# Sums of split mixing weights formed on chip instead of through a scratch tensor, with a new instruction order

## The chip, the cores and the metric

The kernel runs on one core of one Trainium2 chip. The metric is the device time of one execution in microseconds (us). Its engines are TensorE (PE in the profile; its weight loads are PEld), VectorE (DVE), ScalarE (ACT), GpSimd (POOL) and SyncE (SP), which here issues every DMA.

## The reference

The input is `q`, `k`, `v` of 4 batches, 8 heads, 768 positions and 64 columns per head. A local attention (window of 16, plus one key per block of 32 that is the block's maximum, with the block's mean as value) gives `x` of shape 4 x 768 x 512. Then:

```python
theta = x @ w_theta
zr, zi = x * cos(theta), x * sin(theta)
y = einsum('ts,bsd->btd', w_tok_r, zr) + einsum('ts,bsd->btd', w_tok_i, zi)
u = x + y
out = u + maximum(u @ w_ch, 0)
```

The four weights arrive as 64-bit floats and are converted to float32 on chip.

## The kernel before

**Stages.** A batch has 6 tiles of 128 positions, so there are 24 tiles. For one tile TensorE makes the scores (L523), VectorE masks them and takes the row maximum (L559), ScalarE takes the exponential (L563), TensorE transposes (L572) and multiplies by the values (L546), the result is normalised into `xn`, and TensorE turns it (L605) into `x`. The `theta` product is L639 for the first six tiles (plain float32) and L644 for the rest, where each operand is split into a high part that fits the fast matmul format and a low part with the remainder; three products then stand for one. The phases are L655 (ScalarE), L657 (VectorE), an absolute value (L661 or L663) and two sines (L667, L668), and L674 multiplies by `xn` into the tile pair `zu`. ScalarE loads a table whenever it changes between exponential and sine.

**Mixing.** `y` is a sum over 6 steps `s` of `zr`, `zi` times the weights `w_tok_r`, `w_tok_i` of that step. Batches 0 and 1 do it in L702 (first with plain `zu` and float32 weights, then with split operands `hl`). Batches 2 and 3 do it with seven products of half-size blocks, L817 (the function `mix_fast`). Four of the seven need sums of weight blocks. `weight_sums` makes these once: for each of six steps and two halves of the columns it builds a tile `f` with four quarters, does four small adds or subtractions in place (L730, 128 x 192 each), splits the result in high and low (L309/L311 and L318) and writes both to the DRAM tensor `s_scratch`. `mix_fast` streams them back into the second half of the six weight slots `wt`, one load for each step and product, 24 in each of the two batches.

**Where the sums start from.** In the kernel before, each step's whole float32 weights (both kinds, 768 KB) are written from their slot to the DRAM tensor `f_scratch` when they are converted, and `weight_sums` reads them back by halves of the columns (12 loads). Later the same weights are split into the slots `w_t[s, 0]` and `w_t[s, 1]`, high part and low part, for L702 and L817.

**End.** `swap_pools` closes the attention's memory pool; `channel_weights` and `out_batch` then do the last product, again with seven block products (L922), with corrections on VectorE (L929, L941) and one output DMA for each half row.

**Order.** Nothing is scheduled at run time. The constant `ORDER` lists all operations (2292 before) by number; a letter after a number names the engine where there is a choice (`g` GpSimd, `d` VectorE). Each engine carries out its own operations in this order and waits on semaphores for the others. Where a GpSimd operation that shares a port with VectorE stands directly after a VectorE operation of that kind in the list, it also waits for that one's end.

The operation that both the sums and the corrections use is

```python
def add_op(dst, x, y, n, sign, reads, writes, due, engines=("DVE", "POOL")):
```

Of the kernel before, what the change touches and what calls it, by code (L numbers as in the profile page):

```python
# [58 lines left out]
253 104 85 98 215 214 110 223 216 296g 258 224 99d 225 243 255 257 217 118 348g 226 105 227 218 119g 220d 293 256 245 219d 106
244 246 228 247 250 111 120 221 291 121 249 222d 248 123 124g 297 229 122 349g 298 345 259 230 260 262 292 299 261 270 130 125  # L60
301 350g 115 300 271 263 126 272 303 423g 305 302 304 306 273 267d 308 131g 307 116 264d 419 310 135 268 309 265 274 313 127
136g 132 311 312 266d 141 275 269d 314 276 133 315 142g 137 317 316 277 138 352 143 112 231 325 326 318 232 134 327 163 233g
139 144 353 361 168 319d 356 328 320 329 362 278 330 322 355 234 169g 145 331 346 164g 321d 279 364 323 363 282 117 146 324
283 420 332 354 113 347 284 280 365 474 285 147 380 358 114 357 339 165 360 148 366 359 337 166 367 338 149 167 170 368 150
152 381 424 369 422 333 370 400 153 382 128 383 384 171 334 154 172 155 157 281 158g 156 425 385 371 402 401 159 372 386 340
174 335 175g 373 426 392 394 374 421 160 375 377 376 378 387 529 161 404 176 388 379 403 705g 389 454 177 530 179 395 393 178
180 455 456 390g 472 408 457 181 405 182 410 183 427 703 458 459 414 466 409 412 460 461 462 463 411 435 428 467 429 704g 406
437 706g 438 415 431 430 441 468 615g 469 413 436 434 464g 707 521 442 433 465 432 416 417 407 479g 440 564d 523 443 439 480
288g 741 709g 534 444 446d 418 481 535 482 445 485 483 447 490 477 129 492 491 484 475 448 478g 493 486 496 449 451d 532 710g
452 743 450d 488 531g 522 453d 497 616g 487 536 509 537 539 494 586 476d 540 489 538 495 498 510 621 499 391g 501 543 500d 541  # L70
742 511 502 512 545 503 506 513 542 547 551 504 546 733 507 583 289g 286g 708g 549 505d 550 533g 343g 548 544 745 508d 514 744
552 553 515 341 554 555 524 516 556d 517 711 712 518 287g 713d 714 739 585 336g 557 344g 398 734 587 596 558d 599 519 624 588
603 559 715 592 589 716 746 717 561 668 568 591 562 565g 622 735 593 718 566 719 584 560d 597 140 601 720 595 563 598 567 600
602 399g 784 590 594 623 342 569 785d 604 473g 721 786 740 605 572 625 607d 570 634 606 576 608 626 635 787g 617 788 653g 722
618 665 638 151 789 629 574 697 637 630 396d 397g 470 619 525g 723g 737 639 627 790 698g 609d 620 636 628 520 832 612 633 736
471g 162 641 833g 654g 659g 613 738 834g 631 791 640 610 611d 632 792 614d 655 841 642 747 752 643 835g 669 526 644d 793 645
670 646 812 678 672 657 679 650 813d 671 173 667 683 681 658 814d 815 680 663 647d 836 673 748 842 816 675 664 684 843g 817
656 648 818 755 754 724 945g 837 674 682 844 819 660g 677 661 649d 651 666 527d 652 676 685 820 686 687 794 839 689 821 688d
795 838g 756 1015 757 690 528g 571 845g 975 765 662 822 759 760 976d 850 691 840 977d 578 846 978 851g 796 768 823 727d 763
184 797 852 946 699 766 758 692 853g 769 1020 701 694d 979 940 702 980 700 941 847g 772 848 693d 579 981 825 767 695 749 696d  # L80
761 762 771 731 753 750 764 580g 798d 824 982 728 770 732 773 983 774 775d 984 947 956 581g 776 854g 777 995 948 729 778d 959
849 781d 949 950 958 725g 582g 802 952 803 996 997 998 953 799g 859 751 943 1016 1021 779 951 782 855 999 730 780 1074 1000
985 860g 1001 856 800 726 963 1018 808 857 1002 942 954 861g 957 961 960 962 801 955 575 826g 783 964 862 863g 1077 858 944g
965 1003 1022 966 1004 986 967d 864g 968 1005 806 804 1017g 810 1031 972 868 805 865g 1050 828 1023 1051d 1052 1032 869g 573
577 987 829 1170 1053 830 1024 866 1025 1033 989g 1006 969d 1054 827 1035 1037 831 1029 1055 870 1028 993 871 1056 1007g 970
872g 1027 1034 867 973 1120d 1038 1008 877 994 1036 1026 1057 1019d 1058 1013 1030 971 1014 974d 873d 1059 1039 874g 1040 1042
1078 878 1041d 809 811 990g 1079 1043 1047d 1208 1076 807 1087 1089 991 876 992 1209 1088 1090 1011 1210d 1083 1094 1093 1044d
1060 879 1009 880 1211 1080 1212 875 881 1082 1129 1012 1045 882g 1048 1213 886 1061 1126 1081 1092 1066 883 1075 1010 884
1084 1091 1214 1063g 1085 887 1067 885 1062 1127 1121 1046d 988 888 1215 1086 1173 1068 1049 1216 895 1095 1096 1098 1106g
1130 1217 1097d 889 1099 1218d 1279 1107g 1280 1281g 1069 1131 1070 896 1071 1228 1133 1100d 1282 1064g 1219 1135 890 1103d  # L90
1229 1283 1072 1073 1139 1065 891g 1137 1132 1110 1141 892 1142 1101 1284 1111 897 1143 1104 1285 1134 1138 1102d 898g 1108
1105d 1145 899g 1146 1286 1140 1144 1136 1109 1287 1128 893 900d 1158d 1147 1148 901g 1150 894 1288 1172 1250 1149d 1118 1174
1289 1114 1175 1112 1151 1305 1116 1178 1179 902 1202 1236 1122 1152 1183 903 1221g 1123 1306 1124 1185 1307 1308g 1187 1177
1181 1309 1153 904 1182 1160 1184 1232 1310 1155 1189 1237 1230 1233 1220g 1188 1176 1125 1186 1311 905 1156 1162 1171 1290
# [1028 lines left out]
```

## Time and profile before

| | |
|---|---|
| runs | 436.08, 436.68 and 437.91 us (median 436.68) |
| profiled execution, first to last instruction | 435.6 us |
| profiled execution's own time | not listed apart; the median run is 1.1 us above the span |
| busy: PE, DVE, ACT, POOL | 421.7, 352.2, 280.3, 209.7 us |
| moved by DMA | 100.07 MB |

A row of a timeline gives start, duration, engine, line, operation, tiles, and in brackets the idle time just before it on its engine with what ended it; PE rows run into each other because matmuls are pipelined. A row of a group gives busy time, then the mean duration of one in ns, then idle time before them.

### The profile page before, as it was taken

How to read it: one execution, taken by the hardware profiler on the slowest of the kernel's cores; microseconds unless marked ns; L12 is line 12 of the kernel's file. 1: busy time of each engine (PE TensorE's matmuls, PEld its weight loads, DVE VectorE, ACT ScalarE, POOL GpSimd, SP SyncE). 2: the span in 40 equal slices, each digit the busy share in tenths (PEclk: the TensorE clock that was granted, in tenths of full speed). 3: DMA queues.
4: the chain of work that ended last, by engine and by line, in shares of the span. 5: the costliest groups of instructions: out<-in, count | busy, mean ns of one | idle time of the engine just before them, and what ended most of it. 6: DMA issues, size and time to landing. Idle time of an engine off the chain costs nothing.

```text
span 435.6 us, 10044 instructions
## 1 busy us (share of the span) xinstructions
PE 421.7 (97%) x3682; PEld 350.9 (81%) x3682; DVE 352.2 (81%) x947; ACT 280.3 (64%) x600; POOL 209.7 (48%) x208
## 2 busy tenths in 40 slices
PE   5989999998999999999999999999999989999996
PEld 1455555665888888888888899999899989999996
DVE  3799999778988777875757695866489989999996
ACT  1799995787757784866785885493955447455210
POOL 3543324687775665245465578624453410251542
PEclk9899999999999999999999999999999999999999
DMA  8999956989678678848767987883379696220138
GB/s 294 347 354 364 295 197 208 290 257 322 230 233 273 197 224 266 259 139 247 232 188 223 292 273 218 245 246 119 111 230 338 229 367 223 75 73 20 65 136 289
DMA packets 76321, 100.07 MB, mean 230 GB/s; under 512 B 23024, under 2 KB 58864, under 8 KB 76272
## 3 DMA queue, kind: packets, MB, share of 16 engines
q1 hardware_dynamic: 76272, 99.43, 71.1%
q8 instruction: 29, 0.48, 0.5%
q14 instruction: 20, 0.16, 0.1%
HBM read 75.82 MB, written 23.59 MB: 228 GB/s over the span
## 4 chain that ended last, share of the span: by engine, by line
PE 87%; DMA 10%; DVE 1%; ACT 1%; SPq 0%; issue 0%; POOL 0%; DVEq 0%
PE m L702 25%; PE m L817 19%; PE t L644 11%; PE c L922 7%; PE m L922 6%; PE pa L546 5%; PE s L523 4%; PE t L639 3%; PE t L605 3%; DMA q<-qg 3%; PE pa L572 3%; DMA wth<-wth 2%; DMA wt<-wti 2%; DMA zu<-kT 2%; DMA wt<-s_scratch 1%; PE t L922 1%
## 5 line engine op out<-in xcount | busy, mean ns | idle before, releaser
L817 PE MATMUL m<-wt,hl 128*128 128x384 f32 x504 | 95.7, 339 | 1.4 <-DMA wt<-s_scratch 1.2
L817 PEld LDWEIGHTS m<-wt,hl 128*128 128x128 f32 x504 | 87.7, 188 | 4.9 <-ACT hl L309 1.5
L702 PE MATMUL m<-wt,hl 128*128 128x512 f32 (+1 forms) x432 | 84.9, 341 | 0.0
L702 PEld LDWEIGHTS m<-wt,hl 128*128 128x128 f32 x432 | 68.6, 188 | 10.8
L563 ACT ACTIVATE e<-e,st 128x118 f32<-128x118 f32 x192 | 63.1, 388 | 12.1 <-DVE st L559 11.6
L559 DVE CUSTOM_DVE_ANT_0 e<-s,cs 128x118 f32<-128x118 f32 x192 | 46.8, 272 | 9.6 <-PE s L523 4.7
L318 POOL TENSOR_TENSOR hl<-zu,hl 128x512 fp32r<-128x512 f32 x23 | 30.1, 1309 | 43.9 <-DMA wt<-s_scratch 15.9
L644 PE MATMUL t<-wth,xh 128*128 128x512 f32 x144 | 45.3, 396 | 0.0
L674 POOL TENSOR_TENSOR zu<-xn,zu 128x512 f32<-128x512 f32 x20 | 27.0, 1350 | 20.3 <-ACT zu L668 5.5
L657 DVE SCALAR_TENSOR_TENSOR zu<-zu,t 128x512 f32<-128x512 f32 x24 | 16.4, 684 | 24.4 <-ACT zu L655 24.4
L702 PE MATMUL m<-wt,zu 128*128 128x512 f32 (+1 forms) x96 | 33.4, 491 | 1.2 <-DVE zu L674 1.2
L655 ACT ACTIVATE zu<-t,bmagic 128x512 f32<-128x512 f32 x24 | 16.5, 687 | 23.9 <-PE t L644 18.3
L309 ACT CAST hl<-zu 128x512 fp32r<-128x512 f32 x31 | 19.1, 619 | 18.2 <-PE m L817 14.9
L702 PEld LDWEIGHTS m<-wt,zu 128*128 128x128 f32 x96 | 17.5, 190 | 15.8 <-issue 12.6
L546 PEld LDWEIGHTS pa<-v,e 118*64 118x64 f32 x768 | 24.8, 137 | 6.8 <-issue 3.0
L318 DVE TENSOR_TENSOR hl<-zu,hl 128x512 fp32r<-128x512 f32 x37 | 27.6, 751 | 2.3 <-ACT hl L309 2.1
L523 PE MATMUL s<-k,q 64*64 64x118 f32 x768 | 25.6, 272 | 3.9 <-POOL cs L340 3.2
L546 PE MATMUL pa<-v,e 118*64 118x65 f32 x768 | 28.1, 224 | 1.2 <-ACT e L578 1.2
L730 POOL TENSOR_TENSOR zu<-zu 128x512 f32<-128x512 f32 x15 | 21.4, 1432 | 15.0 <-DVE zu L730 4.9
L644 PE MATMUL t<-wth,xl 128*128 128x512 f32 x72 | 28.6, 397 | 0.0
L674 DVE TENSOR_TENSOR zu<-xn,zu 128x512 f32<-128x512 f32 x28 | 24.7, 884 | 4.8 <-ACT zu L668 4.6
L523 PEld LDWEIGHTS s<-k,q 64*64 64x64 f32 x768 | 20.2, 135 | 9.2 <-POOL cs L343 4.0
(181 smaller groups left out, 909.9 us busy)
## 6 DMA issues: line engine op xcount, KB each, us to landing
wt<-s_scratch SPq DMA_DIRECT2D x48, 384.0 KB, 4.4
v<-vg SPq DMA_DIRECT2D x48, 195.0 KB, 5.3
s_scratch<-f SPq DMA_DIRECT2D x24, 384.0 KB, 3.9
k<-kg SPq DMA_DIRECT2D x18, 376.0 KB, 5.5
q<-qg SPq DMA_DIRECT2D x24, 256.0 KB, 6.0
wt<-wtr SPq DMA_DIRECT2D x6, 768.0 KB, 11.0
wt<-wti SPq DMA_DIRECT2D x6, 768.0 KB, 11.4
f<-kT SPq DMA_DIRECT2D x12, 384.0 KB, 4.3
```

Source lines behind the costliest of these rows:

```text
L309: nc.scalar.copy(dst(), src())
L318: lambda e: V[e].tensor_tensor(dst(), src(), hi().bitcast(F32), op=ALU.subtract), reads, writes, due, port=BOTH)
L523: mm(0.79 * len(pairs) / NP, [lambda p=p, g=g, h=h: nc.tensor.matmul(sc[h].get()[ROW[g], p], q.get()[ROW[h], p, ROW[g]], k.get()[ROW[h], p ...
L546: mm(2 * 0.433 + scores[0] + (0.2 if scores[0] else 0.0), [lambda n=n, g=g, a=a: nc.tensor.matmul(xa[a].get()[ROW[g], n], turned[g].get()[ ...
L559: op({"DVE": 0.205}, lambda eng, n=n: nc.vector.tensor_tensor_reduce(e()[:, n], sc[n % 2].get()[:, 2 * a + n // 2], mask(m), -SCALE, 3.0e3 ...
L563: op({"ACT": 0.288}, lambda eng, n=n: nc.scalar.activation(e()[:, n], e()[:, n], AF.Exp, bias=st.get()[:, n:n + 1], scale=-1.0), [(st, n)] ...
L644: calls = [lambda t=t, xx=xx, k=k, c=c: nc.tensor.matmul(th.get(), xx.get()[:, c], w_th[c].get()[:, k], start=(c == 0 and t == 0), stop=(c ...
L674: op({"DVE": c_dve(DM, "two"), "POOL": c_pool(DM)}, lambda e, z=z, hc=hc: V[e].tensor_tensor(z(), xn[b, i].get().rearrange("p h d -> p (h ...
L702: nc.tensor.matmul(acc[th](), zz, w[:, TT[th]], start=(s == 0 and r == 0 and t == 0 and (th == 0 or c == 0)), stop=(s == NT - 1 and r == 1 ...
L730: lambda e: V[e].tensor_tensor(dst(), x(), y(), op=ALU.add if sign > 0 else ALU.subtract), reads, writes, due, port=BOTH)
L817: calls = [lambda ref=ref, tt=tt, z=z, s=s, j=j, t=t, x=x, k=k, bank=bank, first=first: nc.tensor.matmul(bank[j].get()[:, :HT], z.get()[:, ...
L922: calls = [lambda k=k, t=t, x=x, y=y: nc.tensor.matmul(to.get(), weights[n][x][0]()[:, k, j * P:(j + 1) * P], operands[n].get()[:, y, k], ...
```

## The change

1. `f_scratch` is gone, with its 6 writes (768 KB each) and 12 reads (384 KB each).
2. `weight_sums` makes the whole weights again by adding the high and low parts of `w_t[s, r]`: two adds of 128 x 384 for each of 12 tiles, 24 in all. They are `add_op`s, free to stand on VectorE or GpSimd; the list puts 14 on VectorE and 10 on GpSimd.
3. `combine` in `out_batch` names the pool swap among its inputs.
4. `ORDER` is another list: 2298 operations, all of them rearranged, and many elementwise operations on another engine.

```diff
@@ ORDER
-17g 8 0g 1g 31 23 27 25 9 24 18 29 10 28 2 26 39 3 19 32 30 20 4 44g 33 5 6g 190g 49g 46 45 48 7 50 86 194g 47 193 51 60 61 34
+27 17 0g 23 11 18 25 31 24 26 29 8g 9 44 46 10 12 1 2 39 33 28 79 35 45g 19 20 21 3 22 4 48 5 49 32 6g 7g 30 47 184g 93 186g
...
-    f_dram = nc.dram_tensor("f_scratch", (NT, P, 2 * S), F32, kind="Internal").ap()
...
-                dma(lambda f=f: f.get().rearrange("p (q c) -> p q c", q=4),
-                    lambda s=s, cols=cols: f_dram[s].rearrange("p (q c) -> p q c", q=4)[:, :, cols], S * 512, [("fd", s)],
-                    [(f, n) for n in range(4)], 1e6, HT * 2, 0.6, 0.55)
+                for r in range(2):
+                    part = lambda x, s=s, r=r, cols=cols: w_t[s, r].get()[:, x].bitcast(F32).rearrange("p (h c) -> p h c", h=2)[:, :, cols]
+                    add_op(lambda f=f, r=r: f.get().rearrange("p (q c) -> p q c", q=4)[:, 2 * r:2 * r + 2], lambda part=part: part(0),
+                           lambda part=part: part(1), HT, 1, [(w_t[s, r], 0), (w_t[s, r], 1)], [(f, 2 * r), (f, 2 * r + 1)], 1e6)
...
-            add_op(t.get, x[0], y[0], S, -1, x[1] + y[1], [t], due)
+            add_op(t.get, x[0], y[0], S, -1, x[1] + y[1] + ["cpool"], [t], due)
...
-            if j % 2 and K["STR"] < B:
-                pr.key = ("FD", j // 2)
-                dma(lambda s=j // 2: f_dram[s].rearrange("p (r c) -> p r c", r=2), two.get, 2 * S * 512, [(two, 0), (two, 1)], [("fd", j // 2)], 1e6, 6144, 0.55, 0.9)
```

Three places of the new order follow. The first is SyncE's queue at the start of the program. The four loads `zu<-kT` are the keys of the first batch, two head pairs in each `zu` tile; the first scores wait for them. Before:

```order
L303 DMA x_82<-vn 128x2x512
L303 DMA zu_84<-kT 128x798
L303 DMA zu_86<-kT 128x798
L303 DMA zu_84<-kT 128x798
L303 DMA zu_86<-kT 128x798
L303 DMA q_101<-qg 128x512
L303 DMA x_82<-vn 128x2x512
L303 DMA wth1_139<-wth 128x1024
L303 DMA x_82<-vn 128x2x512
L303 DMA wth0_163<-wth 128x1024
L303 DMA q_180<-qg 128x512
L303 DMA wth2_183<-wth 128x1024
```

Now, on the same queue from its first load:

```order
L303 DMA zu_75<-kT 128x798
L303 DMA zu_81<-kT 128x798 x2
L303 DMA x_87<-vn 128x2x512
L303 DMA zu_75<-kT 128x798
L303 DMA q_107<-qg 128x512
L303 DMA x_87<-vn 128x2x512
L303 DMA wth0_111<-wth 128x1024
L303 DMA x_87<-vn 128x2x512
L303 DMA wth2_139<-wth 128x1024
L303 DMA q_143<-qg 128x512
L303 DMA v_179<-vg 96x520
L303 DMA v_183<-vg 96x520
```

Three of the four key loads stand ahead of the first value load, and one `zu` tile is complete after three loads; the third theta weight has moved behind two loads of `v`.

The second is GpSimd about a fifth into the program, where the mixing goes over from plain to split weights (`wt<-wt` on L318 is the low part of a 128 x 768 weight). Before:

```order
L674 TENSOR_TENSOR zu<-xn,zu 128x2x256
L318 TENSOR_TENSOR wt<-wt 128x768
L311 CAST wt<-wt 128x768
L318 TENSOR_TENSOR wth_972<-xh,wth_972 128x512
L495 COPY v<-vs 24x520
L311 CAST wt<-wt 128x768
L318 TENSOR_TENSOR wt<-wt 128x768
L674 TENSOR_TENSOR zu<-xn,zu 128x2x256
L318 TENSOR_TENSOR wt<-wt 128x768
L318 TENSOR_TENSOR hl<-zu,hl 128x512
L318 TENSOR_TENSOR wt<-wt 128x768 x2
```

Now, in the same part of GpSimd's program:

```order
L318 TENSOR_TENSOR hl<-zu,hl 128x512
L405 TENSOR_SCALAR f<-f 128x768
L318 TENSOR_TENSOR wth_1267<-xh,wth_1267 128x512
L674 TENSOR_TENSOR zu<-xn,zu 128x2x256 x2
L730 TENSOR_TENSOR f<-wt 128x384 x2
L730 TENSOR_TENSOR f<-f 128x192 x2
L311 CAST xh<-x 128x512
L674 TENSOR_TENSOR zu<-xn,zu 128x2x256
L730 TENSOR_TENSOR f<-f 128x192
L674 TENSOR_TENSOR zu<-xn,zu 128x2x256
L311 CAST wt<-wt 128x768
L674 TENSOR_TENSOR zu<-xn,zu 128x2x256
```

Most low parts of weights have left GpSimd (8 of 11 stood there before, 3 now), and two of the new adds (`f<-wt`) stand here.

The third is TensorE behind the last `theta` tile, up to the first operand that is made from that tile (`hl_4515` before, `hl_4523` now). Before, from the last `theta` matmul:

```order
L644 MATMUL t_4441<-wth3_1011,xl_4430 128x512
L817 MATMUL m1_4213<-wt_1832,hl_4408 128x384 x3
L817 MATMUL m2_4231<-wt_1832,hl_4408 128x384 x3
L817 MATMUL m0_4472<-wt_1007,hl_4425 128x384 x3
L817 MATMUL m0_4472<-wt_1214,hl_4425 128x384 x3
L817 MATMUL m1_4486<-wt_1007,hl_4425 128x384 x3
...
L817 MATMUL m2_4508<-wt_1235,hl_4418 128x384 x3
L817 MATMUL m0_4472<-wt_912,hl_4432 128x384 x3
L817 MATMUL m1_4486<-wt_1726,hl_4515 128x384 x3
```

Now, from the last `theta` matmul:

```order
L644 MATMUL t_4456<-wth3_450,xl_4453 128x512
L818 MATMUL m2_4482<-wt_984,hl_4291 128x384 x3
L818 MATMUL m2_4482<-wt_1072,hl_4291 128x384 x3
L818 MATMUL m1_4496<-wt_971,hl_4321 128x384 x3
L818 MATMUL m2_4482<-wt_837,hl_4443 128x384 x3
L818 MATMUL m0_4439<-wt_1134,hl_4464 128x384 x3
...
L818 MATMUL m1_4496<-wt_1134,hl_4464 128x384 x3
L818 MATMUL m1_4496<-wt_1487,hl_4464 128x384 x3
L818 MATMUL m0_4439<-wt_1740,hl_4523 128x384 x3
```

Between the last `theta` matmul and the first use of its result stand 12 rows of three matmuls before and 10 now.

## Rows read from the trace of the kernel before

**Rows 1.** The page: busy us, share of the span and instructions by engine.

```profile
PE 421.7 (97%) x3682; PEld 350.9 (81%) x3682; DVE 352.2 (81%) x947; ACT 280.3 (64%) x600; POOL 209.7 (48%) x208
```

**Rows 2.** Windows: stretch, its us, busy PE, PEld, DVE, ACT, POOL, PEclk, DMA share, GB/s.

```profile
0.00:17.00 17.00, 12.36 (x50) 4.14 (x50) 8.04 (x31) 6.56 (x18) 6.62 (x23) 0.90 0.90 326
17.00:45.00 28.00, 25.36 (x360) 15.89 (x360) 26.77 (x103) 25.95 (x58) 12.58 (x21) 1.00 1.03 348
45.00:80.00 35.00, 35.00 (x182) 19.91 (x180) 33.71 (x70) 30.11 (x67) 12.07 (x13) 1.00 0.72 231
80.00:110.00 30.00, 28.63 (x383) 19.43 (x382) 23.31 (x91) 23.38 (x54) 22.59 (x20) 1.00 0.93 296
110.00:180.00 70.00, 70.00 (x706) 59.53 (x706) 56.72 (x182) 49.02 (x110) 42.69 (x41) 1.00 0.75 234
180.00:240.00 60.00, 60.00 (x590) 51.16 (x590) 39.79 (x128) 41.25 (x89) 31.51 (x31) 1.00 0.73 216
240.00:320.00 80.00, 80.00 (x798) 72.27 (x797) 55.12 (x177) 55.28 (x129) 44.22 (x41) 1.00 0.71 215
320.00:370.00 50.00, 48.58 (x275) 47.26 (x274) 47.70 (x75) 26.29 (x43) 13.97 (x11) 1.00 0.83 283
370.00:435.60 65.60, 61.81 (x354) 61.32 (x352) 61.06 (x98) 22.45 (x39) 23.50 (x14) 0.99 0.31 110
```

**Rows 3.** Timeline of TensorE in the first 45 us.

```profile
10.92 1.78 PE L523 MATMUL s<-k,q 64*64 64x118 f32 x32 [3.25 <-POOL cs L340]
12.63 4.53 PE L450 MATMUL pa<-x,vt 128*24 128x512 f32 x8
17.09 1.04 PE L523 MATMUL s<-k,q 64*64 64x118 f32 x32
```

**Rows 4.** DMA issues by line (KB each, us to landing).

```profile
v<-vg SPq DMA_DIRECT2D x48, 195.0 KB, 5.3
...
f_scratch<-wt SPq DMA_DIRECT2D x6, 768.0 KB, 7.3
f<-f_scratch SPq DMA_DIRECT2D x12, 384.0 KB, 4.3
```

**Rows 5.** Groups of line 730 by form, and ScalarE's table loads.

```profile
L730 POOL TENSOR_TENSOR zu<-zu 128x512 f32<-128x512 f32 x15 | 21.4, 1432 | 15.0 <-DVE zu L730 4.9 <-DVE hl L318 4.6 <-DVE zu L663 3.6
L730 POOL TENSOR_TENSOR f<-f 128x192 f32<-128x192 f32 x25 | 18.5, 745 | 16.1 <-DMA f<-f_scratch 5.2 <-DVE f L730 5.1 <-DVE xl L318 3.4
L563 ACT ACT_TABLE_LOAD x13 | 16.7, 1283 | 0.2
L730 DVE TENSOR_TENSOR zu<-zu 128x512 f32<-128x512 f32 x15 | 12.8, 863 | 0.1
L730 DVE TENSOR_TENSOR f<-f 128x192 f32<-128x192 f32 x23 | 10.2, 444 | 0.8 <-POOL f L730 0.7
```

**Rows 6.** Timeline around 100 us, three engines.

```profile
97.55 1.83 POOL L318 TENSOR_TENSOR wt<-wt 128x768 fp32r<-128x768 f32 x1
97.62 2.30 DVE L674 TENSOR_TENSOR zu<-xn,zu 128x512 f32<-128x512 f32 x1
99.98 1.34 PE L702 MATMUL m<-wt,zu 128*128 128x512 f32 x3 [1.23 <-DVE zu L674]
```

**Rows 7.** Timeline behind the last theta tile.

```profile
326.02 8.16 PE L817 MATMUL m<-wt,hl 128*128 128x384 f32 x46
326.22 0.69 ACT L655 ACTIVATE zu<-t,bmagic 128x512 f32<-128x512 f32 x1 [3.03 <-PE t L644]
329.88 1.29 DVE L674 TENSOR_TENSOR zu<-xn,zu 128x512 f32<-128x512 f32 x2
331.33 0.69 DVE L318 TENSOR_TENSOR hl<-zu,hl 128x512 fp32r<-128x512 f32 x1 [0.16 <-ACT hl L309]
```

**Rows 8.** Chain of waits and timeline where batch 3 streams its sums.

```profile
345.49 5.85 DMA wt<-s_scratch
351.48 2.32 PE L817 MATMUL m<-wt,hl 128*128 128x384 f32 x12 [1.20 <-DMA wt<-s_scratch]
```

More of the change, by code (lines that the diff above doesn't have):

```diff
@@ L59 @@
[L59 to L94, printed above, removed]
@@ new lines @@
+884 1120 1155 1180 1181 1156 1157 1158d 1313d 1182 1224d 1159 1185 1289 1290 1291 1123 1314g 889 890 891 892d 893g 894 895
+1292 1128 1129 1130 1189 1131 1678 1225 1183 1191 1190 1194 1168 1293 1192 1166 1167 1294 1226g 1315 1316 1169 1295 1296
+1227g 1170g 1164 1171 1195 1246 1255 1165 1184 1187 896 897 1248 1297 1599g 1247 1186 898g 1317 1318 899 1298 900 901 1605
+1606g 1174 1160 1161 1162 1249 1188 1163d 906 1196 1193 907 1178 1330 1319 908g 902 903 1175 1320 1321 1212 1213 1172 1173
+1210 1331 904 1197 1198 905 1244 1200 1199d 1257 1201 1205 1202d 1600g 909g 1203 1204 910g 1360 1228g 1229g 1266 1361 1268
@@ new lines @@
+1998 2003 2075 2238 2061 2001 2124 2004 2079 2134 2127 2076 2082 2062 2158 2077 2068 2128 2071g 2069g 2120 2080 2006 2164
+2005 2093 2078 2047 2083 2094d 2096 2098 2099 2090 2125 2086 2084 2121 2179g 2100 2131 2097 2165 2103 2091 2087 2101 2126
+2107 2108 2104 2196 2217 2122 2162 2132 2092 2180g 2123 2189 2239 2088 2133g 2129 2130 2137d 2138 2111 2141 2112 2105 2277
+2181 2109 2110 2240g 2159 2163d 2194 2247 2187 2143 2254 2171 2160 2161 2139 2191 2195g 2140 2167 2135 2142 2172 2249g 2085
+2182 2146 2147 2168 2150 2154 2151 2201 2144 2169 2173 2175 2148 2155 2192 2256 2183 2197 2188 2170 2145 2222 2190 2152 2198
@@ new lines @@
+2257 2248 2199 2203 2218 2244 2202 2200 2102 2224 2206 2241g 2263 2176 2219 2207 2208 2214 2242 2193 2174 2220 2204 2245
+2251g 2221 2246g 2223 2225 2210 2177 2211 2264 2149 2231 2227 2228 2153 2243g 2261 2215 2235 2229 2258 2232 2252 2212 2278
+2233 2089 2236 2284 2285 2282 2259 2205 2260d 2279 2262 2113 2253g 2280 2156 2166 2250g 2255g 2286 2270 2081 2271 2230 2281
+2283 2234 2266 2267 2216 2268 2237 2226 2287 2288 2289 2265 2209 2272 2291 2292 2293 2269 2106 2290 2273 2295 2296 2274 2275
+2213 2294 2297 2276
```

120 lines of the change are left out of this document (71 added, 49 removed).

## The prediction

> **What bounds the kernel now.** I read the page's busy shares first, then a table of windows by stage, then the waits of TensorE alone. TensorE is busy for 421.7 of 435.6 us [rows 1]. The windows tell where the other 13.9 us lie [rows 2]: 4.64 in the first 17 us, 2.64 up to 45, nothing from 45 to 80, 1.37 from 80 to 110, nothing at all from 110 to 320 (210.00 busy in 210.00), 1.42 from 320 to 370 and 3.79 in the last stretch, nearly all of which is the tail behind the last matmul (add, output DMA). So TensorE sets the time from about 45 us on. An edit elsewhere is worth something only if it reaches one of these holes, or opens a new one. The start is another regime: there the DMA share is 0.90 and then 1.03, VectorE is busy for 26.77 of 28 us and ScalarE for 25.95, so loads and conversions set the pace.
>
> The matmuls are the same in number and shape in both kernels, so TensorE's own 421.7 us stay but for slow-clock time and switches between kinds of matmul. All of the forecast is in the holes.
>
> **The change part by part.** *The scratch tensor.* 6 writes of 768 KB and 12 reads of 384 KB go [rows 4], 9.4 MB of 100, with 18 issues on SyncE. Who waited for them? GpSimd alone, before its small adds, 5.2 us in all [rows 5], in a stretch where TensorE never waits. Worth 0. The most it could be is the 1.4 us hole at 80 to 110 us, where the first writes ran; the wait that ends that hole is another one (below).
>
> *The 24 adds.* No row has an add of 384 columns on two SBUF operands. The nearest are 192 and 512 columns: 444 and 863 ns on VectorE, 745 and 1432 ns on GpSimd [rows 5]. By columns between them, 0.70 and 1.16 us, so 14 x 0.70 = 9.7 us (6.2 to 12.1) and 10 x 1.16 = 11.6 us (7.5 to 14.3). They stand where `weight_sums` stood, mostly between 110 and 240 us. There VectorE is idle for 13.3 + 20.2 = 33.5 us and GpSimd for 27.3 + 28.5 = 55.8 us [rows 2], which is the cover. Worth 0; should an add stand ahead of something urgent, it costs one hole of about the size of that at 100 us, so 0 to +1.2.
>
> The rows show a price that this sum leaves out. At 97.62 us a multiplication on VectorE took 2.30 us beside a GpSimd operation of 1.83 us, where two of the same form with GpSimd quiet took 1.29 together [rows 6, 7]; TensorE waited 1.23 us for it. The Trainium skill says the same as a rule (SBUF — State Buffer, on the shared port pair): the pair is locked for a whole instruction and the loser blocks fully. By it each of the 10 GpSimd adds could hold up VectorE for its own length, a rule that speaks against this change; with the bound above that would be 11.6 us of VectorE, still inside its 33.5 us, but it raises the chance of the slow rival below.
>
> *The hole at 100 us.* It ends on that delayed multiplication. Its other party was the low part of a 128 x 768 weight on GpSimd. In the new order only 3 of these 11 stand on GpSimd instead of 8, and between the theta tile in question and its first use TensorE has one more group of three theta matmuls of 512 columns, about 0.7 us (3 x 0.177 x 512 / 384, from the 46 matmuls in [rows 7]). On the other side, part of the multiplications `zu<-xn` of that tile have moved to GpSimd, where new adds also stand. I take -0.9; from -1.2 (hole gone) to +1.0 (one more delay of 2.30 - 0.65 = 1.65 us less 0.7 us of added cover).
>
> *The start.* The first scores began at 10.92 us after a hole of 3.25 and ran slowly: 1.78 us for 32, against 1.04 at 17.09, and the eight value matmuls behind them took 4.53 [rows 3]. The mean granted clock of this stretch is 0.90 [rows 2], so part of it ran at the 1.2 GHz level after the idle time. In the new queue one `zu` tile of keys is complete after three loads, not four, the reductions follow the tiles, and the five warm-up matmuls stand together at the very start. That may bring the scores forward by about 1 us and save the 0.74 us by which they were slow: up to -3.3, the hole itself, if all of it were kept. But VectorE, ScalarE and the DMA queues limit the 28 us that follow, and the third theta weight has moved back behind two loads of `v`, 195 KB each [rows 4]: 0.40 MB, at 348 GB/s [rows 2] 1.2 us. The gain in front is mostly lost there: I take -0.5, from -3.3 to +1.2.
>
> *Behind the last theta tile.* From the theta's end to the low part of its first operand 331.33 + 0.69 - 326.2 = 5.8 us passed [rows 7]; TensorE had 12 rows of three matmuls at 8.16 / 46 = 0.177 us [rows 7], 6.4 us, and did not wait. Now there are 10 rows, 5.3 us. The first two of the operand's matmuls can start on the high part, so +0.3; from 0 to +1.1.
>
> *The stream of batch 3.* The load of 345.49 took 5.85 us and TensorE waited 1.20 us [rows 8]. The same six slots are refilled by the same loads right behind one another, so the wait stays: 0, from -1.4 to +1.4. *The end.* VectorE is nearly full there (61.06 of 65.6 us), the new order has taken some casts and splits off it, and TensorE's last product is again followed by one add and one store: 0 +/- 0.5.
>
> **The sum.** 0 + 0 - 0.9 - 0.5 + 0.3 + 0 + 0 = -1.1 us. The profiled execution's span is 435.6 and the median run 1.1 above that; 434.5 of span and 1.1 around it make 435.6 us.
>
> **The rivals.**
> *Crowding at the changeover (slower).* Between the first plain mixing matmul and the first split one the new list puts 99 operations on ScalarE instead of 89, with 7 table loads instead of 5, and 127 on VectorE instead of 112, since weight splits have come over from GpSimd and are made earlier. That stretch was 45 to 110 us, where ScalarE was busy for 53.5 of 65 us and VectorE for 57.0 [rows 2], 0.60 and 0.51 us for one operation. Ten and 15 more are 6.0 us (2.6 of them the two table loads, [rows 5]) and 7.6 us, of idle times of 11.5 and 8.0: VectorE keeps 0.4 us of cover in 65. It decides once VectorE is later than the 6 to 7 us that TensorE has between a theta tile and its use; then three or four of the tiles there each cost a hole of 1.2 us: +4 on the sum, 439.6. For it: the full VectorE at 45 to 80 us (33.71 of 35). Against: the theta blocks stand together now and leave long unbroken mixing behind them.
> *The start keeps its gain (faster).* If the earlier scores carry through to the first mixing matmul, -3.0 instead of -0.5: 433.1. For it: TensorE is idle for 7.3 us in the first 45 and two of its warm-up matmuls there only fill time. Against: the DMA share of 1.03.
> *The sums come late (the change costs what it should save).* The sums now need the splits of both weights and not the bare weights. If the last sum reaches `s_scratch` later than the stream wants it, TensorE waits once in 240 to 270 us for the write and the load behind it, each about the 4.3 us of such a load [rows 4], less what the mixing in front covers: about +4, 439.6. Against: the list ends the sums at about the same mixing step as before.
>
> **How the numbers follow.** TensorE-bound with the holes about as now has 0.51, the kept start 0.24, the crowding 0.20, the late sums 0.05. The first one's own range is 433.5 to 438.0 from its bounds taken half at a time. The range that holds eight in ten goes from 432.4 to 440.2. A change below 0.5% (434.5 to 438.9) can't be told from none. Faster gets 0.24 and a third of the first case's part near 435.6 (0.15), so 0.39; slower gets most of the crowding and late sums and a little of the first case, 0.23; the rest is 0.38.
>
> **What would show it.** Right: TensorE busy for 420 to 422 us, nothing idle between 110 and 320 us, at 80 to 110 us a hole under 1 us, a wait of about 1.2 us for `wt<-s_scratch` near 350 us, the first scores before 10.5 us but the first mixing matmul at 45 to 46. Wrong: several waits of TensorE on VectorE or ScalarE at 60 to 110 us (crowding), the first mixing matmul before 43.5 us (kept start), a wait on `wt<-s_scratch` at 250 to 270 us (late sums), or any new wait of the attention's matmuls on `k`, `q` or `v`.

## The result, and the profile after

The changed kernel takes 439.06 us (median of 9 runs, 437.09 to 440.61), the kernel before 435.90 in the same comparison (9 runs): ratio 1.0072, 95% interval [1.0047, 1.0097]. A second comparison gave 440.14 to 435.00 us, 1.0109 [1.0080, 1.0139]. So it is slower by about 0.9%, where 435.6 us was forecast.

Executions of the changed kernel lie between 436.6 and 440.8 us and the profiles kept of it are of 436.6 to 437.6, so a stage is read below from them and from one kernel with the same order up to 365 us whose profiled execution took 440.2 us (e14).

The page and the windows of the changed kernel (stretch, its us, busy PE, PEld, DVE, ACT, POOL, PEclk, DMA share, GB/s), execution of 437.61 us, span 435.9, beside [rows 1, 2]:

```profile
PE 423.4 (97%) x3682; PEld 349.9 (80%) x3682; DVE 360.4 (83%) x952; ACT 295.0 (68%) x606; POOL 212.4 (49%) x218
...
0.00:17.00 17.00, 13.01 (x62) 4.53 (x64) 9.45 (x33) 6.91 (x19) 7.11 (x25) 1.00 0.91 313
17.00:45.00 28.00, 25.02 (x358) 15.84 (x353) 26.05 (x92) 25.31 (x56) 11.74 (x20) 1.00 1.04 325
45.00:80.00 35.00, 35.00 (x253) 20.92 (x252) 32.89 (x90) 30.75 (x66) 13.96 (x15) 1.00 0.82 262
80.00:110.00 30.00, 30.00 (x322) 20.29 (x321) 27.74 (x97) 28.53 (x63) 16.44 (x20) 1.00 0.72 206
110.00:180.00 70.00, 70.00 (x711) 59.75 (x710) 58.53 (x166) 51.88 (x107) 38.36 (x39) 1.00 0.54 164
180.00:240.00 60.00, 60.00 (x586) 50.77 (x585) 42.98 (x142) 43.54 (x97) 34.64 (x35) 1.00 0.72 211
240.00:320.00 80.00, 80.00 (x794) 71.89 (x793) 58.13 (x175) 57.71 (x125) 49.17 (x45) 1.00 0.68 205
320.00:370.00 50.00, 48.95 (x269) 45.97 (x268) 47.92 (x79) 26.00 (x42) 10.38 (x9) 1.00 0.79 273
370.00:435.90 65.90, 61.42 (x347) 59.95 (x345) 56.67 (x88) 24.39 (x40) 30.65 (x16) 0.99 0.28 101
```

The hole at 80 to 110 us is gone (30.00 of 30), nothing is idle from 45 to 320, and the first 17 us are busier. By these columns the kernel should be faster. Two things speak against it: TensorE is busy for 1.7 us more with the same matmuls, and in the last stretch GpSimd has 30.65 us of work instead of 23.50 while VectorE has 56.67 instead of 61.06.

Busy time can't tell where a TensorE that is always busy loses time. A second measure can: give each form of matmul one fixed duration (0.173 us for 128x384, 0.232 for 128x512, and so on, from these traces), add them up in the order in which they start (403.1 us in each of these kernels), and take TensorE's *lag*: the start of a matmul less the work in front of it. A table of its growth by stage of work, worked out from all matmul records (us; the last row is the span). Only differences along a row mean something:

| work done, us | before | before again (e4) | changed | changed (e9) | e14 | e12 | e13 |
|---|---|---|---|---|---|---|---|
| 0 to 50 | 17.82 | 17.11 | 16.48 | 15.43 | 17.09 | 18.09 | 16.81 |
| 50 to 90 | 3.15 | 3.01 | 1.45 | 1.45 | 1.51 | 1.45 | 1.58 |
| 90 to 300 | 4.67 | 4.60 | 5.46 | 5.78 | 6.05 | 5.79 | 4.39 |
| 300 to 330 | 2.15 | 1.42 | 2.49 | 2.55 | 3.82 | 2.69 | 0.71 |
| 330 to 370 | 0.40 | 0.41 | 2.25 | 1.97 | 2.27 | 1.74 | 0.41 |
| 370 to the end | 4.25 | 4.27 | 4.60 | 4.57 | 4.60 | 4.41 | 4.27 |
| span | 435.6 | 434.0 | 435.9 | 434.9 | 438.5 | 437.3 | 431.3 |

Against the kernel before, the changed kernel gains 1.6 us at the hole and up to 2.4 at the start. It loses 0.8 to 1.4 in the long mixing and 0.3 to 2.4 in the last mixing stage. From 330 to 370 us of work it loses 1.6 to 1.9; up to 0.6 of that, by the execution, still belongs to the mixing stage, whose last load from `s_scratch` is used at 335 us of work. What is left, with the 0.3 behind 370, is the output product: 1.6 us, alike in the four profiles of the changed kernel (this one, e3, e9 and e10).

The rows that answer to [rows 3, 5, 7, 8] (timeline of TensorE at the start; line 730 and table loads by form; behind the last theta tile; the stream of batch 3 and, new, the output product):

```profile
10.38 1.04 PE L523 MATMUL s<-k,q 64*64 64x118 f32 x32
11.49 1.90 PE L450 MATMUL pa<-x,vt 128*24 128x512 f32 x4
14.12 1.90 PE L450 MATMUL pa<-x,vt 128*24 128x512 f32 x4 [0.73 <-DMA x<-vn]
...
L730 DVE TENSOR_TENSOR f<-f x22: 318/352/1450, 126.6 to 261.7; 128x192 f32<-128x192 f32 x22
L730 DVE TENSOR_TENSOR f<-wt x14: 540/550/2864, 126.9 to 250.5; 128x384 f32<-128x384 f32 x14
L730 POOL TENSOR_TENSOR f<-wt x10: 997/1018/1812, 99.6 to 242.2; 128x384 f32<-128x384 f32 x10
...
326.06 0.69 ACT L655 ACTIVATE zu<-t,bmagic 128x512 f32<-128x512 f32 x1 [1.35 <-PE t L644]
330.91 0.69 DVE L318 TENSOR_TENSOR hl<-zu,hl 128x512 fp32r<-128x512 f32 x1 [0.16 <-ACT hl L309]
336.90 1.28 DVE L318 TENSOR_TENSOR hl<-zu,hl 128x512 fp32r<-128x512 f32 x2
...
350.57 1.32 PE L818 MATMUL m<-wt,hl 128*128 128x384 f32 x6 [0.38 <-DMA wt<-s_scratch]
359.94 2.37 PE L818 MATMUL m<-wt,hl 128*128 128x384 f32 x12 [0.26 <-DMA wt<-s_scratch]
393.04 0.97 PE L923 MATMUL c<-wt,wth 128*128 128x384 f32 x4 [0.60 <-DVE wt L318]
```

The middle group gives ns as least, median and most. An add of 384 columns takes 0.55 us on VectorE and 1.02 on GpSimd in the median, up to 2.86 and 1.81 at worst. The two rows `hl<-zu,hl` end at 331.60 and 338.18 us, and TensorE's lag steps up behind them, from 331.66 and 338.23, by 0.34 and 0.63 us, though the timeline shows hardly any idle time there. The last row is new: the kernel before has no wait in the output product. What VectorE and GpSimd did ahead of it (timelines of both engines, changed kernel):

```profile
383.82 3.70 DVE L730 TENSOR_TENSOR cb<-cu,cb 128x768 f32<-128x768 f32 x2
390.17 1.01 DVE L930 TENSOR_TENSOR zu<-m,zu 128x384 f32<-128x384 f32 x2
391.10 1.88 DVE L318 TENSOR_TENSOR wt<-cb,wt 128x768 fp32r<-128x768 f32 x1
392.90 0.95 DVE L318 TENSOR_TENSOR wt<-x,wt 128x768 fp32r<-128x768 f32 x1
394.24 0.95 DVE L318 TENSOR_TENSOR wt<-cb,wt 128x768 fp32r<-128x768 f32 x1
...
384.86 1.85 POOL L318 TENSOR_TENSOR wt<-x,wt 128x768 fp32r<-128x768 f32 x1 [2.47 <-DVE cb L730]
390.33 1.84 POOL L730 TENSOR_TENSOR cb<-x 128x768 f32<-128x768 f32 x1 [3.62 <-DVE wt L318]
394.49 2.41 POOL L318 TENSOR_TENSOR wt<-cb,wt 128x768 fp32r<-128x768 f32 x1 [2.32 <-DVE cu L942]
```

One such operation takes 0.95 us with GpSimd quiet (392.90). Beside the GpSimd operation of 384.86 two of them took 3.70, beside the one of 390.33 one took 1.88, and TensorE's wait ends when it ends. Where VectorE's operation began first (394.24) it kept its 0.95, and the GpSimd operation behind it took 2.41. This is the collision of [rows 6], at another place.

The kernel before has such collisions at its end too, but fewer. A sum tells how many: over VectorE's operations on two tensors behind 370 us that began beside a GpSimd operation already under way, the time beyond what the same form takes with GpSimd quiet (its hold-up). It is 2.1 us in both profiles of the kernel before and 5.2 us in three of the changed kernel (this one, e3 and e9).

### The profile page after: what moved, and what is told of

The parts are those of the page before. It is cut to its first block, busy times and chain, and to the rows that moved or that the text cites. A ratio compares the mean times of both kernels' runs of the same rounds, so it can differ in the third digit from the quotient of the medians.

```text
span 435.9 us, 10050 instructions
## 1 busy us (share of the span) xinstructions
PE 423.4 (97%) x3682; PEld 349.9 (80%) x3682; DVE 360.4 (83%) x952; ACT 295.0 (68%) x606; POOL 212.4 (49%) x218
## 4 chain that ended last, share of the span: by engine, by line
PE 83%; DVE 8%; DMA 6%; issue 1%; ACT 1%; SPq 0%; DVEq 0%; POOL 0%; POOLq 0%; ACTq 0%
PE m L702 25%; PE m L818 16%; PE t L644 11%; PE pa L546 6%; PE c L923 6%; PE s L523 5%; PE t L639 4%; PE m L923 4%; PE pa L572 3%; PE t L605 3%; DMA wt<-wti 2%; DMA wt<-s_scratch 2%; DMA zu<-kT 1%; PE t L923 1%; DVE hl L318 1%
## 5 line engine op out<-in xcount | busy, mean ns | idle before, releaser
L818 PE MATMUL m<-wt,hl 128*128 128x384 f32 x504 | 94.6, 340 | 1.0 <-DMA wt<-s_scratch 0.6
L818 PEld LDWEIGHTS m<-wt,hl 128*128 128x128 f32 x504 | 87.0, 188 | 4.9 <-DMA wt<-s_scratch 1.3
L702 PE MATMUL m<-wt,hl 128*128 128x512 f32 (+1 forms) x432 | 79.9, 340 | 0.0
L702 PEld LDWEIGHTS m<-wt,hl 128*128 128x128 f32 x432 | 66.9, 188 | 10.1
L559 DVE CUSTOM_DVE_ANT_0 e<-s,cs 128x118 f32<-128x118 f32 x192 | 45.8, 273 | 9.8 <-PE pa L546 5.0
L674 POOL TENSOR_TENSOR zu<-xn,zu 128x512 f32<-128x512 f32 x22 | 30.4, 1388 | 31.0 <-ACT zu L668 12.9
L318 POOL TENSOR_TENSOR hl<-zu,hl 128x512 fp32r<-128x512 f32 x23 | 30.9, 1348 | 23.5 <-ACT hl L309 11.0
L318 DVE TENSOR_TENSOR hl<-zu,hl 128x512 fp32r<-128x512 f32 x37 | 27.8, 758 | 3.9 <-ACT hl L309 2.2
L730 POOL TENSOR_TENSOR zu<-zu 128x512 f32<-128x512 f32 x14 | 18.5, 1331 | 23.5 <-DVE hl L318 11.6
L644 PEld LDWEIGHTS t<-wth,xh 128*128 128x128 f32 x144 | 25.7, 188 | 5.1
L309 ACT CAST hl<-zu 128x512 fp32r<-128x512 f32 x33 | 20.3, 618 | 13.1 <-PE m L818 11.5
L730 POOL TENSOR_TENSOR f<-f 128x192 f32<-128x192 f32 x26 | 17.8, 685 | 15.6 <-DVE f L730 8.5
```

Source lines behind the costliest of these rows:

```text
L309: nc.scalar.copy(dst(), src())
L318: lambda e: V[e].tensor_tensor(dst(), src(), hi().bitcast(F32), op=ALU.subtract), reads, writes, due, port=BOTH)
L559: op({"DVE": 0.205}, lambda eng, n=n: nc.vector.tensor_tensor_reduce(e()[:, n], sc[n % 2].get()[:, 2 * a + n // 2], mask(m), -SCALE, 3.0e3 ...
L644: calls = [lambda t=t, xx=xx, k=k, c=c: nc.tensor.matmul(th.get(), xx.get()[:, c], w_th[c].get()[:, k], start=(c == 0 and t == 0), stop=(c ...
L674: op({"DVE": c_dve(DM, "two"), "POOL": c_pool(DM)}, lambda e, z=z, hc=hc: V[e].tensor_tensor(z(), xn[b, i].get().rearrange("p h d -> p (h ...
L702: nc.tensor.matmul(acc[th](), zz, w[:, TT[th]], start=(s == 0 and r == 0 and t == 0 and (th == 0 or c == 0)), stop=(s == NT - 1 and r == 1 ...
```

## The experiments

Hybrids of the two orders are made by taking one list up to a place and then what is left of the other in its own order. Line numbers shift by one or two between kernels, as the list is longer or shorter.

**Noise, and more profiles.** e3, e9 and e10 are the changed kernel, e4 the kernel before, with no edit.

> The changed kernel as it is, once more, beside a second profile of before: the size of the loss and where it stands in a typical execution. Theory and rival alike: ratio 1.005 to 1.010. If the loss is spread over the stages (crowding of the engines), TensorE's lag behind its own work grows evenly from 110 to 350 us against before; if it is one wait, the lag steps up by 1 to 3 us in one place.

> The kernel before, unchanged, for a second profile and for the noise of the comparison: ratio 0.998 to 1.002 by every theory.

> The changed kernel again, for one more profile, since both earlier profiles (437.0 and 437.6 us) lie below its median of some 439.5 us. If this one is of 439 us or more: theory (the gain of the start is not repeated in every execution: transfers and VectorE land differently there) puts 1 us or more of the difference before 100 us of the span; rival (late transfers of the last mixing stage) puts it between 300 and 360 us.

> As the run before it: one more profile of the changed kernel, with the same two readings of an execution of 439 us or more.

e3: 1.0109 [1.0080, 1.0139]; e4: 0.9999 [0.9981, 1.0017]; e9 and e10: 436.61 and 436.89 us, so the long execution that they were to catch was missed. In e3's profile the lag grows by 8.4 us between 90 and 330 us of work against 6.0 in e4's, in many pieces, and steps up by 1.3 from 360 to 366: both readings of e3 hold in part.

**Sums and order apart (e1, e2).**

```diff
 ORDER of the kernel before; in weight_sums as in the changed kernel:
+ the two adds of a half right in front of its first small sum
--- and e2
 ORDER of the changed kernel, without the 24 adds:
+ 6 writes to f_scratch, 12 loads, each 4 to 20 places ahead of its first reader
```

> The kernel before's order of all its instructions, with the sums made on chip as in the changed kernel: the f_scratch transfers are gone and the two adds of each half stand right before the first small sum that reads them, on the engines that the changed kernel gives them. Theory (the new order costs the time, the sums are free): about 435.9 us, as before, ratio 0.999 to 1.002. Rival A (the 24 adds cost it: they lengthen the operand chain on VectorE and GpSimd and the matmuls wait): 438 to 440 us, ratio 1.005 to 1.010, with new idle time of TensorE before products of the operands made after 110 us.

> The changed kernel's order with the sums fetched from f_scratch as before: 6 writes and 12 loads on SyncE's queue, no adds (the loads are issued 4 to 20 places ahead of their first reader in the written order). Theory (the new order costs the time): 438 to 441 us, ratio 1.005 to 1.012, as the changed kernel. Rival A (the adds cost it): 434.5 to 436.5 us, ratio 0.997 to 1.002. A load that lands late would show as idle time of VectorE before a small sum and is to be told apart by that.

Neither theory held: e1 446.07 us, 1.0249 [1.0222, 1.0276]; e2 463.81 us, 1.0658. Both lists were spoilt by the splice: in e1 the adds lengthen the path in front of urgent work (TensorE waits 1.2 us for `st` and 1.0 for `e`, both from VectorE; a third wait of 1.2, for `zu`, is the old hole), in e2 GpSimd waits 15.8 us for VectorE before its small sums (8.5 in the changed kernel). They don't tell sums and order apart. In e1 the 24 adds, some 21 us on two engines, go with 11 us of time: in a list that has no room for them they are not free.

**The adds alone (e8).**

```diff
-    add_op(f[2r:2r+2], high part of w_t[s, r], low part of w_t[s, r], ...)   # twice
-    small sums of q[x], q[y]
+    small sums of the high parts of w_t
```

> The changed kernel without its 24 new adds: the small sums read the upper halves of the weights in their place, so the sums lack the lower halves; everything else and its order is the same. Theory of crowding (the adds take VectorE and GpSimd time that the operands of 110 to 330 us need): 1.5 to 3 us less than the changed kernel, 436.5 to 438 us, ratio 1.002 to 1.007. Rival (the adds are free and the order alone loses the time): 439 to 441 us, ratio 1.008 to 1.014.

438.16 us, 1.0059 [1.0037, 1.0081], the ratio of its theory; the changed kernel has 1.0072 and 1.0109, and the intervals overlap. The windows of 110 to 320 us, e8 and then e9:

```profile
110.00:320.00 210.00, 210.00 (x2089) 182.63 (x2088) 149.99 (x467) 152.07 (x323) 112.91 (x110) 1.00 0.64 192
...
110.00:320.00 210.00, 209.96 (x2084) 182.07 (x2083) 159.78 (x481) 152.22 (x322) 121.35 (x117) 1.00 0.64 191
```

9.8 us of VectorE and 8.4 of GpSimd less, and TensorE's lag from 90 to 300 us grows by 5.24 instead of 5.78. By the profiles the adds cost 0.2 us (changed) to 0.5 (e9) of TensorE's time in this stage, by the two ratios 0.13 and 0.50% in the runs; 0.59% is left without them, so most of the loss is in the order.

**The end of the list (e7, e6, e12).**

```diff
 e7:  first 1907 words of the list before, then the rest as in the changed kernel (with f_scratch)
 e6:  first 1918 words of the changed list, then the rest as before
 e12: first 2061 words of the changed list, then the rest as before
```

> The kernel before whose order from about 335 us of the span on is that of the changed kernel. Theory: 1.0 to 2.0 us over before, 436 to 437.5 us, ratio 1.002 to 1.005. Rival: as before, ratio 0.998 to 1.002.

> The changed kernel whose order from about 335 us of the span on is that of the kernel before. Theory (1.4 us of the loss stands at the first matmuls of the output product, which wait for operands that VectorE makes, and up to 0.7 us in the mixing stream ahead of it): 437 to 438.3 us, ratio 1.004 to 1.008. Rival (the wait there is paid for elsewhere, at the end of the span): 439 to 441 us, as the changed kernel.

> The changed kernel whose order from about 365 us of the span on is that of the kernel before: a later seam than in the first such kernel, which spent 2.2 us in one wait at its seam near 345 us. Theory (1.4 us of the loss are the waits of the output product at 390 us, where VectorE's operations run beside one of GpSimd): 437 to 438.2 us, ratio 1.003 to 1.007, and no wait of TensorE on VectorE near 390 us. Rival (VectorE is behind there whatever the order): 439 to 440.5 us and a wait of 0.5 us or more at another place of the output product.

e7, the kernel before with the new end: 438.22 us, 1.0063 [1.0036, 1.0091], more than its theory's 0.2 to 0.5%, where the changed kernel lost 0.72 and 1.09%. Its waits of TensorE behind 60 us (us in total, times, longest):

```profile
PE m L703 <- DVE zu L675: 1.2, 1, 1.2
PE m L818 <- ACT hl L310: 1.0, 1, 1.0
PE m L818 <- DVE x L827: 0.8, 1, 0.8
PE c L923 <- DVE wt L319: 0.6, 1, 0.6
```

The first is the old hole at 100 us, and the last, at 393 us, is the changed kernel's own. The two between them, at 345 and 353 us, are not: there the changed kernel has no wait on ScalarE and one of 0.2 us on `x`, so they come with the splice, and e7's time says too much. e6, the other way round (438.30 us, 1.0074 [1.0049, 1.0099], as its theory said), lost 2.2 us in one wait at its splice at 345 us. The lag looks past both splices: from 330 to 370 us of work it grows by 1.78 us in e7 and by 0.45 in e6, against 0.40 in the kernel before and 1.97 and 2.25 in the changed kernel. The sum of VectorE's hold-ups behind 370 us goes the same way: 5.2 us in e7, 2.4 in e6. So the end costs the time.

e12 (1.0048 [1.0027, 1.0069], 437.88 us) has the old end from 365 us on: no wait near 390 us, hold-ups of 1.9 us, and a ratio 0.2 to 0.6% below the changed kernel's two, as its theory said (its interval overlaps the first of theirs and lies below the second). But from 335 to 370 us of work the lag of its profile still grows by 1.3 us, in smaller steps, the largest at 382 us, against 1.7 in the changed kernel and 0.4 before. So the rival, that the wait would only move, holds in part; why the earlier splice of e6 is free of these steps was not traced.

**GpSimd beside VectorE (e14, e13).** Two GpSimd operations of the changed kernel's end, and one of the kernel before at 97 us, are given to VectorE and stand a few places later in the list.

```diff
 e14
-... 2084 2121 2179g 2100 2131 2097 ... 2132 2092 2180g 2123 2189 ...
+... 2084 2121 2100 2131 2179 2097 ... 2132 2092 2123 2180 2189 ...
 e13
-... 557 344g 398 734 587 596 558d 599 519 624 ...
+... 557 398 734 587 596 558d 599 519 344 624 ...
```

> The changed kernel; two operations of 128x768 that GpSimd makes at 384.3 us (wt<-x, 1.85 us) and 389.7 us (cb<-x, 1.84 us) are given to VectorE, each one or two places later in the written order. Theory (VectorE's 128x768 operations at 383 to 392 us take 1.8 us each beside GpSimd and 0.95 us alone): the wait of 0.6 us ahead of the output product near 392 us goes, 0.7 to 1.3 us less than the changed kernel, ratio to before 1.004 to 1.008. Rival (VectorE is full there, and the two operations delay it): the wait stays or grows, ratio 1.009 to 1.014.

> The kernel before; one subtraction of 128x768 (wt<-wt), which GpSimd makes at 96.7 us in 1.83 us while VectorE's 128x512 addition beside it takes 2.30 us, is given to VectorE behind that addition. Nothing else is changed. Theory (the addition is slow because GpSimd works beside it, so that VectorE is done earlier although it has one operation more): the addition takes 0.7 to 0.8 us, TensorE's wait of 1.25 us there goes, and the kernel takes 434.0 to 434.9 us, ratio 0.996 to 0.999. Rival (VectorE has no room there: its extra 0.95 us makes later operations late): ratio 1.000 to 1.004.

e14: 440.00 us, 1.0099 [1.0073, 1.0126], no gain. The timelines (VectorE, GpSimd, TensorE) tell why:

```profile
386.07 2.01 DVE L731 TENSOR_TENSOR cb<-cu,cb 128x768 f32<-128x768 f32 x2
392.53 0.95 DVE L319 TENSOR_TENSOR wt<-cb,wt 128x768 fp32r<-128x768 f32 x1
396.04 2.49 DVE L319 TENSOR_TENSOR wt<-cb,wt 128x768 fp32r<-128x768 f32 x1 [0.36 <-ACT wt L310]
...
395.85 1.86 POOL L319 TENSOR_TENSOR wt<-cb,wt 128x768 fp32r<-128x768 f32 x1 [10.80 <-DVE cu L943]
...
393.83 1.22 PE L924 MATMUL c<-wt,wth 128*128 128x384 f32 x6
399.52 1.31 PE L924 MATMUL m<-wt,wth 128*128 128x384 f32 x6 [1.31 <-DVE cu L943]
```

The two that took 3.70 take 2.01, the one of 1.88 takes 0.95, and the wait at 393 us is gone: from 360 to 366 us of work the lag grows by 0.10 us, against 1.31 in the changed kernel and 0.12 before. The next GpSimd operation now begins just before the next subtraction (395.85 and 396.04) and not behind it, that subtraction takes 2.49 us, and TensorE waits 1.31 us there. The theory is right in its mechanism and wrong in its forecast, and the ratio is the rival's: the collision moved on. The rival's reason, that VectorE is too full for two more operations, is not shown: the wait is shorter than the 1.54 us by which that subtraction was held up.

e13: 433.76 us, 0.9964 [0.9946, 0.9983], faster than both kernels, as its theory said. Timelines around 97 us (VectorE, GpSimd, TensorE), against [rows 6]:

```profile
96.56 0.69 DVE L675 TENSOR_TENSOR zu<-xn,zu 128x512 f32<-128x512 f32 x1
97.17 0.95 DVE L319 TENSOR_TENSOR wt<-wt 128x768 fp32r<-128x768 f32 x1
98.19 1.29 POOL L319 TENSOR_TENSOR hl<-zu,hl 128x512 fp32r<-128x512 f32 x1 [1.67 <-DVE wt L319]
97.52 1.46 PE L703 MATMUL m<-wt,zu 128*128 128x512 f32 x4
```

VectorE's multiplication (the expectation calls it an addition) takes 0.69 us instead of 2.30. It has done both operations 1.56 us after it began the first, where before the first alone took 2.30, and the hole of 1.23 us is gone.

**The start (e5, e11, e15 to e18).**

```diff
 e5, e11: first 650 (712) words of the changed list, then the rest as before (with f_scratch)
 e15:     first 266 words of the list before, then the rest as in the changed kernel; e16: and e14
 e17 (e18: and e12), loads only; four later loads change places too
-27 17 0g 23 11 18 25 31 24 26 29 ...
+31 17 0g 23 11 18 27 25 24 26 29 ...
```

> The kernel before, with f_scratch and all, whose order is the changed kernel's up to about 100 us of the span (start, changeover and the hole behind it) and the order before from there. Theory (the new order gains some 3 us by 100 us and the stages behind lose it again): 431.5 to 433.5 us, ratio 0.991 to 0.996. Rival (what is gained at the start is given back later whatever the order, because another engine or the transfers pace the stages behind): 434.5 to 436 us, ratio 0.998 to 1.002.

> The kernel before, with f_scratch, in the changed kernel's order up to about 120 us of the span and in its own from there: the seam some 10 us later than in the first such kernel, at a place where the two orders have done nearly the same work. Theory (the new start and changeover gain 1.5 to 3 us and the first such kernel lost them at its seam, in two waits of 1.3 and 1.8 us on VectorE): 432.5 to 434.3 us, ratio 0.993 to 0.998. Rival (the gain is given back behind any seam, because VectorE is behind by then): 435 to 437.5 us, ratio 0.999 to 1.004.

> The changed kernel whose order in the first 45 us of the span is that of the kernel before, its order of loads too. Theory (the new order of loads at the start is late by some 2 us in more than half of the executions): 0.8 to 2 us less than the changed kernel in the median, 437.5 to 438.7 us, and a spread without the gap between 438 and 439 us. Rival (the long executions come from elsewhere): 439 to 441 us, with the same spread.

> The two edits before together, on the changed kernel. By both theories 436.3 to 437.8 us, ratio 1.002 to 1.006; by both rivals 439 to 441 us.

> The changed kernel with its first 14 loads issued in the order of the kernel before (the first load of x<-vn ahead of the four of zu<-kT); the order of all other instructions is the changed kernel's. Theory (the long executions of the changed kernel come of the new order of these loads): 437 to 438.3 us, ratio 1.003 to 1.007, and no gap in the spread between 438 and 439 us. Rival A (landing times at the start vary whatever the order of the loads, and the changed kernel's order of computation stands nearer to them): 439 to 441 us with the same spread. Rival B (the first scores, which wait for the loads of kT, come later): 440 us or more, also in the fastest execution.

> As the run before it, and from about 365 us of the span on the order of the kernel before, which by itself took 1.6 us off the changed kernel (437.88 us). Theory: 435.8 to 437 us, ratio 1.000 to 1.003. Rival A: 437.5 to 438.5 us. Rival B: 439 us or more.

e5: 437.39 us, 1.0033 [1.0013, 1.0054]; e11 447.55; e15 445.83; e16 446.43 us. Each lost what it should show in waits at its splice (1.3 and 1.8 us in e5, 7.5 in e11, 3.6 in e15 and e16) and at the reduced clock behind them, so their times decide nothing. By its lag e5 is 2.2 to 3.1 us ahead of the kernel before at 90 us of work, and loses 5.0 more than it from there to 300. e17: 440.89 us, 1.0125 [1.0104, 1.0146]; e18: 440.01 us, 1.0093 [1.0076, 1.0110]: rival B. The old order of loads under the new order of computation makes the first scores wait (0.33 and 0.47 us for `k`) and is not the cure.

That the start differs from one execution to the next is seen in the same order of loads and of computation. TensorE at the start, e9 (436.61 us) and then e12 (439.02 us):

```profile
8.91 1.90 PE L450 MATMUL pa<-x,vt 128*24 128x512 f32 x4
14.03 1.90 PE L450 MATMUL pa<-x,vt 128*24 128x512 f32 x4 [0.42 <-DMA x<-vn]
...
9.55 1.88 PE L451 MATMUL pa<-x,vt 128*24 128x512 f32 x4 [1.73 <-DMA x<-vn]
15.10 1.90 PE L451 MATMUL pa<-x,vt 128*24 128x512 f32 x4 [0.73 <-DMA x<-vn]
```

VectorE could begin on the second tile of keys at 6.93 us in e9 and at 8.16 in e12, and by 50 us of work e12 is 2.7 us behind. That tile alone does not decide it: in the first profile of the changed kernel VectorE began on it at 6.3 us, and TensorE is 1.1 us behind e9 at 50 us of work. e14 is 1.7 behind there, and in the last mixing stage it waits 0.95 and 0.77 us for `wt<-s_scratch`, together 1.1 us more than e9. By the table the start has 1.7 and the last mixing stage 1.3 of the 3.6 us between the two spans; the long mixing and the end have 0.3 each. That the typical execution of the changed kernel itself is longer at these two places is argued from e12 and e14, since no profile of one was caught. Why loads land later in one execution than in another stays open.

## Why the prediction was wrong, point by point

- **The step that failed** is the last term: *"The end. VectorE is nearly full there, the new order has taken some casts and splits off it ... 0 +/- 0.5."* It was +1.6 us, in every profile of the changed kernel (335 us of work to the end). The operations did leave VectorE (61.06 to 56.67 us), but for GpSimd (23.50 to 30.65, against [rows 2]), and there they hold up VectorE's operations: 3.70 us for 1.90, 1.88 for 0.95, in sum 5.2 us behind 370 us where it was 2.1. I had priced this very collision at 100 us [rows 6] and did not look for it where the change put more GpSimd work beside the fullest VectorE. e6 and e7 show that the place costs the time, e14 that GpSimd's operations make the wait at 393 us. That the time comes back without them is not shown, since e14 lost it again one operation later. The Trainium skill (SBUF — State Buffer, section "SBUF: two separate sides") says that of a VectorE operation with two SBUF inputs and a GpSimd operation that reads SBUF the one that starts first gets the shared port pair and the other blocks; the traces agree (2.30 us behind a GpSimd operation, 0.69 without it, e13; 0.95 ahead of one, at 394.24).
- **Behind the last theta tile, +0.3 (0 to +1.1):** +0.34, at 331 us, by the cause named. A second operand late by 0.63 us, at 338 us, has no term.
- **The stream of batch 3, 0 (-1.4 to +1.4):** from 300 to 335 us of work, less these 0.97, the lag of the changed kernel grows by 2.1 and 1.9 us (e9) and that of e14 by 3.1, the kernel before by 2.2 and 1.4: within its bounds in the two profiles, up to 1.7 in e14. The wait on `wt<-s_scratch` is there as said, 0.38 and 0.26 us in one execution, 0.95 and 0.77 in another (e14). The changed list issues five loads of `cu` behind the load concerned, the list before two; that load took 7.0 us in e14 and 5.1 in e4. That the first causes the second was not tried.
- **Nothing can be lost from 110 to 320 us, since nothing is idle there:** wrong as a premise. Busy is 210.00 of 210.00 in both kernels, yet TensorE loses 0.8 to 1.4 us more between 90 and 300 us of work, in steps of at most 0.4 at switches between kinds of matmul. Summed over the switches alone, the lag grows by 0.5 to 0.6 us more in each profile of the changed kernel and in e8, so that part is the order in which the kinds follow one another; e8 puts 0.2 to 0.5 on the adds. Which switch costs how much was not tried by itself. TensorE's busy time, 420 to 422 us by the prediction, was 423.4 to 424.5.
- **The hole, -0.9 (-1.2 to +1.0):** -1.6, more than its range allowed, right in sign; e13 removes the hole of the kernel before by the cause named.
- **The start, -0.5 (-3.3 to +1.2):** from -2.4 to +1.0 (e12) by the execution, in its range. The first scores came at 10.38 us and ran in 1.04, as said.
- **The adds, 0 (0 to +1.2):** +0.2 to +0.5; their sizes, 0.70 and 1.16 us forecast, were 0.55 and 1.02. **The scratch tensor, 0:** not measured by itself, since e2 failed.
- **The rivals.** Crowding named the right sum, 439.6, and a wrong place: TensorE has no wait between 45 and 110 us. The crowding was at the end of the list, for which no rival stood. The kept start was there by its sign (first mixing matmul at 43.21 to 43.48 us in three profiles, 44.26 in the fourth, 45.65 and 44.95 before), and the time was lost again behind it. Late sums: no wait at 240 to 270 us.
- **The base of the sum.** The 1.1 us put around the span are 1.7 in the runs (437.61 less 435.9, 435.69 less 434.0), so the profile of the kernel before is of an execution of some 437.3 us, 0.6 longer than the median that the sum started from. The range for eight in ten, 432.4 to 440.2, holds both medians of the changed kernel, but by its width: the change went the other way.

In sum: with a start as late as before, e14 against e4, 0.0 - 1.5 + 1.4 + 2.4 + 1.9 + 0.3 = +4.5 us, the difference of their spans; the medians of the changed kernel and the kernel before differ by 3.2 and 5.1. e14's end costs as much as the changed kernel's, at another place. The cause of the 1.6 us at the end is shown; that of the rest is shown in part.

## What to carry to other kernels

Taking an operation off a full VectorE and giving it to GpSimd can make VectorE later, not earlier; where TensorE waits for a VectorE operation of twice its usual length, look at what GpSimd did beside it, and first try that operation on VectorE, behind the urgent one (e13: one word of the list, -0.36%; in e14 the like gained nothing, as the next GpSimd operation collided). When a whole order is exchanged, price the end of the list like its start: there is no later slack that takes up what goes wrong. And a window that shows TensorE busy throughout bounds nothing: compare the work done in it.
